# A soft mixture of experts behind a Fourier layer: the last product on half rows, without zero blocks

## The chip, the core and the metric

The kernel runs on one core of a Trainium2 chip. The core has TensorE (matrix products into PSUM), VectorE, ScalarE and GpSimd (elementwise work; GpSimd is POOL in the profile), and SyncE (SP), from whose queue nearly all DMA transfers are issued here. The engines run side by side and wait for each other on semaphores. The metric is the device time of one execution in microseconds (us); lower is better. The kernel before takes 567.42 us (median of three runs, 566.44 to 567.63).

## The reference

Everything is float32. A Fourier layer comes first; its output is never needed in full, only through the mixture behind it.

```python
X = np.fft.rfft(x, axis=1)                   # x: 8 x 2496 x 256
Yr = Xr @ w_r - Xi @ w_i + b_r
Yi = Xr @ w_i + Xi @ w_r + b_i
Yr, Yi = softshrink(Yr, 0.01), softshrink(Yi, 0.01)
x = np.fft.irfft(Y, n=2496, axis=1).reshape(19968, 256)
logits = x @ phi                             # 32 slots: 8 experts of 4
d = softmax(logits, over tokens)
slot_input = d.T @ x                         # 32 x 256
slot_out[e] = relu(slot_input[e] @ w1[e]) @ w2[e]
c = softmax(logits, over slots)
out = c @ slot_out                           # 19968 x 256
```

The change concerns the last line alone: for each of 19968 tokens, a product of its 32 weights c with the 32 x 256 matrix slot_out.

## The kernel before

For most of its time the kernel works through 8 batches of 2496 tokens: transforms, linear layer, softshrink, logits, and for each batch the weights c, which it writes to device memory (c_dr, batches 0 to 5) or keeps in SBUF (batches 6 and 7). An order by due times on a heap (`at`, `step_to`, `run_until`) decides how the stages of neighbouring batches interleave. Behind the last batch come the two layers of the experts (tiles hps and po) and then the combine, with which the program ends.

The weights for two consecutive tokens lie side by side. c_prep (line 1051) splits a batch's weights into a high part in fp32r, written by ScalarE, and the rest, subtracted by VectorE (tile chl); for a pair of tokens this gives 4 x 32 = 128 values: token 0 high, token 0 low, token 1 high, token 1 low. c_trans (line 1061) transposes them on TensorE (tile pc, 11 groups of at most 117 pairs for each batch, in three steps of 4, 4 and 3) and copies them to the tiles ct. A column of ct is then a pair of tokens, its 128 rows are the values above, and 1248 columns belong to each batch.

The combine walks over 78 blocks of 128 columns (NBLK, line 37). For block j, the 128 columns of ct are the stationary matrix, and two products of 512 columns add up in one PSUM bank, pq: one with rhs[0], the high part of slot_out, one with rhs[1], its low part. Each rhs is 128 x 2 x 256: rows 0 to 63 hold slot_out in columns 0 to 255 and zeros behind, rows 64 to 127 hold zeros and then slot_out, so that columns 0 to 255 of pq are the first token of each pair and 256 to 511 the second. Half of what each product multiplies is zero. PSUM banks for pq come by turns from the pools "pf" and "pl", two banks each.

ScalarE copies the even blocks from PSUM to half of a tile ost, VectorE the odd ones to the other half; there are nine buffers for ost. SyncE writes two blocks at a time to the output, 512 KB, and the first two and last two blocks by themselves, 256 KB each (lines 1198 to 1201).

Between the blocks the loop carries work for later batches: the table todo (line 1176) holds for a block which c_prep and c_trans are recorded behind it, and run_until (line 1202) does the same with the steps for the weights of batch 7. Each engine executes its instructions in the order recorded, so a transpose that waits for its chl holds up the products behind it on TensorE.

Before the loop, lines 1160 to 1173 make rhs: po is split into so[0] and so[1], a product with a mask (prep) puts slot_out onto all rows, and copies of 64 rows each put it into rhs over zeros, which GpSimd wrote at lines 1084 to 1087.

Of the kernel before, what the change touches and what calls it, by code (L numbers as in the profile page):

```python
# [11 lines left out]
F32 = mybir.dt.float32  # L12
F32R = mybir.dt.float32r
# [4 lines left out]
B, N, D = 8, 2496, 256  # L18
# [9 lines left out]
E, F = 8, 1024  # L28
# [7 lines left out]
TR = 128  # L36
NBLK = B * CB // TR
# [146 lines left out]
def fourier_soft_moe_kernel(ctx: ExitStack, tc: tile.TileContext, t: dict, out: bass.AP):  # L184
# [18 lines left out]
    def psum(tag, name):  # L203
        return pp.tile([128, 512], F32, tag=tag, name=name, bufs=psum_bufs[tag])

    def wtile(shape, dt, tag, name):
        if tag in a_bufs:
            return wap.tile(list(shape), dt, tag=tag, name=name, bufs=a_bufs[tag])
        if tag in main_bufs:
            return wmp.tile(list(shape), dt, tag=tag, name=name, bufs=main_bufs[tag])  # L210
        return wcp.tile(list(shape), dt, tag=tag, name=name, bufs=chain_bufs[tag])
# [8 lines left out]
    V, A, P = (_InOrder(tc, e) for e in (nc.vector, nc.scalar, nc.gpsimd))  # L220
# [15 lines left out]
    def sp(**kw):  # L236
        tc.keep_in_program_order(nc.sync.dma_start(**kw))
# [4 lines left out]
    def mm(**kw):  # L242
        tc.keep_in_program_order(nc.tensor.matmul(**kw))  # L243

    def copy(eng, out, in_):
        if eng is nc.scalar or eng is A:
            eng.copy(out=out, in_=in_)
        else:
            eng.tensor_copy(out=out, in_=in_)
# [509 lines left out]
    def run_until(t):  # L759
        while heap and heap[0][0] < t:  # L760
            step_to(heapq.heappop(heap)[2])
# [106 lines left out]
    def hl_tile(name):  # L868
        return pools["tm"].tile([128, F], F32, tag="hl", name=name, bufs=NHL)
# [171 lines left out]
    cts, chls = {}, {}  # L1041
# [19 lines left out]
    def c_trans(b, i0, eng):  # L1061
        ni = min(4, G // 2 - i0)
        pc = psum("pt", f"pc{b}_{i0}")
        x, r = divmod(i0, GX // 2)
        for i in range(ni):
            tc.keep_in_program_order(
                nc.tensor.transpose(  # L1067
                    out=pc[:, i * P1 : (i + 1) * P1],
                    in_=chls[b][x][:, 2 * (r + i) : 2 * (r + i) + 2].rearrange("p g h s -> p (g h s)"),
                    identity=ident[:P1, :P1],  # L1070
                )
            )
        c0 = b * CB + i0 * P1
        c1 = min(c0 + ni * P1, (b + 1) * CB)
        for lo in range(c0 - c0 % F, c1, F):
            u0, u1 = max(lo, c0), min(lo + F, c1)
            if lo not in cts:
                cts[lo] = ta_tile(f"ct{lo}").bitcast(F32R)
            copy(eng, cts[lo][:, u0 - lo : u1 - lo], pc[:, u0 - c0 : u1 - c0])
# [1 line left out]
    at(T_["cl"], c_load, 0)  # L1081
    run_until(TB + 24)

    rhs = []
    for a in range(2):
        rhs.append(wtile([128, 2, D], F32R, "p_sb", f"rhs{a}"))
        P.memset(rhs[a].bitcast(F32), 0.0)
    slz, hz = pools["slz"], pools["hz"]
    hps = [psum("pl", f"hps{h}") for h in range(2)]
    po = psum("pr", "po")  # L1090
# [72 lines left out]
    A.copy(out=so[0], in_=po[:, :D])  # L1163
    V.tensor_tensor(out=so[1], in0=po[:, :D], in1=so[0].bitcast(F32), op=ALU.subtract)
    c_trans(0, 0, V)
    for i, tag, dst in ((0, "ps", ((0, A), (1, A))), (1, "pl", ((0, V),)), (1, "pl", ((1, A),))):
        prep = psum(tag, f"prep{i}")
        mm(out=prep[:, :D], lhsT=dmr, rhs=so[i], start=True, stop=True)
        for a, eng in dst:
            r0 = slice(64 * a, 64 * a + 64)  # L1170
            copy(eng, rhs[i][r0, a, :], prep[r0, :D])
    c_trans(0, 4, V)
    c_trans(0, 8, A)

# [1 line left out]
    todo = {}  # L1176
    for b in range(B - 1):
# [2 lines left out]
            todo.setdefault(at0 + 1, []).append((c_prep, b + 1))  # L1180
        for i0, d, eng in ((0, 4, A), (4, 6, V), (8, 8, A)):
            todo.setdefault(at0 + d, []).append((c_trans, b + 1, i0, eng))
    for j in range(NBLK):
        if j % 2 == 0:
            ost = hl_tile(f"ost{j}")
        pq = psum(("pf", "pl")[j % 2], f"pq{j}")
        lo = j * TR - j * TR % F
        for a in range(2):
            mm(
                out=pq,  # L1190
                lhsT=cts[lo][:, j * TR - lo : j * TR - lo + TR],
                rhs=rhs[a].rearrange("p b d -> p (b d)"),
                start=(a == 0),
                stop=(a == 1),
            )
        half = slice(j % 2 * 512, j % 2 * 512 + 512)
        copy((A, V)[j % 2], ost[:, half], pq)
        if j < 2 or j >= NBLK - 2:
            sp(out=out[j // 2, :, half], in_=ost[:, half])
        elif j % 2:  # L1200
            sp(out=out[j // 2], in_=ost)
        run_until(1000 + 6 * j * TR / CB + 0.1)
        for fn, *args in todo.get(j, []):
            fn(*args)


def OUT_SHAPE():
# [55 lines left out]
```

## Time and profile before

| | us |
|---|---|
| Median of three runs | 567.42 |
| The profiled execution | 563.34 |
| Its span, first to last instruction | 561.5 |
| TensorE busy, over the span | 521.4 |
| VectorE busy | 422.0 |
| ScalarE busy | 298.1 |
| GpSimd busy | 281.1 |

A row of the chain of waits gives a start in us, a time in us and the work (engine, tile, line of the code, count of instructions). In the rows of instruction groups stand line, engine, operation, tiles out<-in, shape, count, busy us and mean ns of one, then the idle time of the engine ahead of them with what ended it. Most work carries the line of a helper (L180, L243), so groups are told apart by tiles. The name pq occurs twice: as a tile of the earlier stages (pq<-rt, pq<-pk) and as the bank of the combine (pq<-rhs,ct). "PEld" is the weight load of a product, and a matmul's "mean ns" is its latency: the pace of a series is its time in the chain divided by its count.

### The profile page before, as it was taken

The numbers are of one execution on the slowest core, as the hardware profiler recorded it, in microseconds if no ns is written. First come the engines' busy times: TensorE is split into PE (matmuls) and PEld (weight loads), VectorE is DVE, ScalarE is ACT, GpSimd is POOL, SyncE is SP. The second block draws the span as 40 slices with busy tenths as digits, with TensorE's granted clock in tenths as the row PEclk, the third lists the DMA queues.
The fourth block names the chain that finished last, engine by engine and source line by source line (L and its number), as shares of the span: only waits on it lengthen the run. The fifth ranks groups of instructions, "written<-read, shape, count | busy, mean of one in ns | idle before, by whom it ended". The sixth has DMA issues, their size and how long they took to land.

```text
span 561.5 us, 11780 instructions
## 1 busy us (share of the span) xinstructions
PE 521.4 (93%) x4354; PEld 442.2 (79%) x4354; DVE 422.0 (75%) x837; ACT 298.1 (53%) x650; POOL 281.1 (50%) x258
## 2 busy tenths in 40 slices
PE   8669999999999999999999999999899979899794
PEld 4458999989898889889988898987687867367573
DVE  0347897799979897989789978986795764248783
ACT  4435555666566656665665666653433333147572
POOL 0037777766766576658655866684554402000100
PEclk9999999999999999999999999999999998999899
DMA  8788464756476637664757474766634378979898
GB/s 301 249 294 292 151 207 152 210 179 170 163 216 207 189 118 208 207 180 167 204 171 199 155 201 167 222 230 178 186 131 126 113 183 276 392 240 368 325 374 351
DMA packets 93684, 121.44 MB, mean 216 GB/s; under 512 B 46786, under 2 KB 68736, under 8 KB 93628
## 3 DMA queue, kind: packets, MB, share of 16 engines
q1 hardware_dynamic: 93372, 119.63, 65.4%
q10 hardware_dynamic: 256, 1.08, 0.5%
q8 instruction: 34, 0.56, 0.4%
q14 instruction: 22, 0.18, 0.1%
HBM read 69.87 MB, written 50.82 MB: 215 GB/s over the span
## 4 chain that ended last, share of the span: by engine, by line
PE 70%; DVE 13%; DMA 10%; ACT 3%; issue 2%; SPq 1%; ACTq 0%; DVEq 0%
PE py L243 16%; PE px L243 11%; PE pq L243 9%; PE pa L243 8%; PE pk L243 7%; PE pt L532 4%; PE pr L243 3%; DMA eb<-ed 2%; PE pc L1067 2%; DMA ad<-ast 2%; PE pe L243 2%; DMA ap<-adr 2%; DVE mx L180 1%; DVE clpL L180 1%; DVE xtl L180 1%
## 5 line engine op out<-in xcount | busy, mean ns | idle before, releaser
L180 POOL TENSOR_TENSOR rt<-ut,rt 128x512 f32<-128x512 f32 x79 | 111.7, 1414 | 24.4 <-DVE rt L180 18.4
L180 POOL TENSOR_TENSOR xsl<-xsm,xsh 128x256 fp32r<-128x256 f32 x77 | 59.3, 770 | 102.4 <-DVE xsh L180 71.0
L180 POOL TENSOR_TENSOR xl<-xr,xh 117x512 fp32r<-117x512 f32 x73 | 98.5, 1350 | 22.6 <-ACT xh L180 14.7
L243 PE MATMUL px<-smov,ap 128*128 128x128 f32 x640 | 85.6, 277 | 8.0 <-DMA ap<-adr 4.5
L243 PEld LDWEIGHTS px<-smov,ap 128*128 128x128 f32 x640 | 80.3, 193 | 13.7 <-issue 8.1
L180 ACT CAST xth<-px 128x512 fp32r<-128x512 f32 x80 | 46.8, 585 | 73.0 <-PE py L243 37.6
L180 ACT COPY ast<-pa 128x512 f32<-128x512 f32 x86 | 50.3, 587 | 64.5 <-PE pa L243 61.6
L180 DVE SCALAR_TENSOR_TENSOR ut<-py,pk,k 128x256 f32<-128x256 f32 x160 | 69.5, 475 | 15.0 <-PE py L243 13.1
L180 DVE TENSOR_TENSOR xtl<-px,xth 128x512 fp32r<-128x512 f32 x80 | 54.6, 682 | 26.8 <-ACT xsm L180 22.0
L243 PE MATMUL py<-xth,nwsh 128*128 128x256 f32 x160 | 53.5, 334 | 0.0
L180 DVE TENSOR_SCALAR rt<-ut 128x512 f32<-128x512 f32 x69 | 52.2, 756 | 0.5
L243 PE MATMUL pk<-xsh,w_rh 128*128 128x256 f32 x160 | 47.9, 300 | 2.0 <-DVE xsh L180 2.0
L180 ACT COPY T<-pt 128x512 f32<-128x512 f32 x70 | 42.1, 601 | 9.0 <-PE pt L532 7.3
L532 PE MATMUL pt<-pk,rt 128*128 128x128 f32 x320 | 45.9, 273 | 0.9 <-DVE dd L180 0.6
L243 PE MATMUL pk<-xsl,w_rh 128*128 128x256 f32 x160 | 45.1, 282 | 0.0
L243 PE MATMUL pk<-xsh,w_rl 128*128 128x256 f32 x160 | 44.9, 281 | 0.0
L243 PE MATMUL py<-xtl,nwsh 128*128 128x256 f32 x160 | 44.7, 279 | 0.0
L243 PE MATMUL py<-xtl,wdh 128*128 128x256 f32 x160 | 44.7, 279 | 0.0
L243 PE MATMUL py<-xth,wdl 128*128 128x256 f32 x160 | 44.7, 279 | 0.0
L243 PE MATMUL py<-xth,nwsl 128*128 128x256 f32 x160 | 44.7, 279 | 0.0
L243 PE MATMUL py<-xth,wdh 128*128 128x256 f32 x160 | 44.7, 279 | 0.0
L243 PE MATMUL pq<-rhs,ct 128*128 128x512 f32 x156 | 43.1, 415 | 0.3 <-DVE ost L180 0.3
(186 smaller groups left out, 1241.7 us busy)
## 6 DMA issues: line engine op xcount, KB each, us to landing
ap<-adr SPq DMA_DIRECT2D x76, 256.0 KB
out<-ost SPq DMA_DIRECT2D x37, 512.0 KB
xr<-in_x SPq DMA_DIRECT2D x35, 512.0 KB
adr<-ast SPq DMA_DIRECT2D x20, 768.0 KB
w<-in_moe_w SPq DMA_DIRECT2D x25, 512.0 KB
adr<-ast SPq DMA_DIRECT2D x8, 512.0 KB
w<-in_moe_w SPq DMA_DIRECT2D x14, 256.0 KB
x<-in_x SPq DMA_DIRECT2D x11, 256.0 KB
```

The lines of the kernel that those rows point to most:

```text
L180: return lambda *a, **k: self.tc.keep_in_program_order(f(*a, **k))
L243: tc.keep_in_program_order(nc.tensor.matmul(**kw))
L532: tc.keep_in_program_order(nc.tensor.transpose(out=out, in_=in_, identity=identity))
L1067: nc.tensor.transpose(out=pc[:, i * P1 : (i + 1) * P1], in_=chls[b][x][:, 2 * (r + i) : 2 * (r + i) + 2].rearrange("p g h s -> p (g h s)") ...
```

## The change

The loop goes over pairs of blocks (j - 1, j). A pair has two banks, one from "pf" for the first tokens and one from "pl" for the second. For each of the two blocks and each of high and low, there are two products of 64 rows and 256 columns: rows 0 to 63 into the first bank, rows 64 to 127 into the second. A rhs is 128 x 256 without zero blocks. ScalarE copies the first bank and VectorE the second, each to the two places in ost that belong to its tokens. All writes are of 512 KB. What todo holds for either block is recorded behind the pair.

```diff
-    rhs = []
-    for a in range(2):
-        rhs.append(wtile([128, 2, D], F32R, "p_sb", f"rhs{a}"))
-        P.memset(rhs[a].bitcast(F32), 0.0)
+    rhs = [wtile([128, D], F32R, "p_sb", f"rhs{a}") for a in range(2)]
...
-    for i, tag, dst in ((0, "ps", ((0, A), (1, A))), (1, "pl", ((0, V),)), (1, "pl", ((1, A),))):
+    for i, tag, eng in ((0, "ps", A), (1, "pl", V)):
         prep = psum(tag, f"prep{i}")
         mm(out=prep[:, :D], lhsT=dmr, rhs=so[i], start=True, stop=True)
-        for a, eng in dst:
-            r0 = slice(64 * a, 64 * a + 64)
-            copy(eng, rhs[i][r0, a, :], prep[r0, :D])
+        copy(eng, rhs[i], prep[:, :D])
...
-    for j in range(NBLK):
-        if j % 2 == 0:
-            ost = hl_tile(f"ost{j}")
-        pq = psum(("pf", "pl")[j % 2], f"pq{j}")
-        lo = j * TR - j * TR % F
-        for a in range(2):
-            mm(
-                out=pq,
-                lhsT=cts[lo][:, j * TR - lo : j * TR - lo + TR],
-                rhs=rhs[a].rearrange("p b d -> p (b d)"),
-                start=(a == 0),
-                stop=(a == 1),
-            )
-        half = slice(j % 2 * 512, j % 2 * 512 + 512)
-        copy((A, V)[j % 2], ost[:, half], pq)
-        if j < 2 or j >= NBLK - 2:
-            sp(out=out[j // 2, :, half], in_=ost[:, half])
-        elif j % 2:
-            sp(out=out[j // 2], in_=ost)
+    for j in range(1, NBLK, 2):
+        ost = hl_tile(f"ost{j}")
+        ov = ost.rearrange("p (k g d) -> p k g d", g=2, d=D)
+        pqs = [psum(tag, f"pq{j}_{g}") for g, tag in enumerate(("pf", "pl"))]
+        for k in range(2):
+            c = (j - 1 + k) * TR
+            lo = c - c % F
+            for a in range(2):
+                for g in range(2):
+                    rows = slice(64 * g, 64 * g + 64)
+                    mm(
+                        out=pqs[g][:, k * D : k * D + D],
+                        lhsT=cts[lo][rows, c - lo : c - lo + TR],
+                        rhs=rhs[a][rows],
+                        start=(a == 0),
+                        stop=(a == 1),
+                    )
+        for g in range(2):
+            copy((A, V)[g], ov[:, :, g, :], pqs[g].rearrange("p (k d) -> p k d", d=D))
+        sp(out=out[j // 2], in_=ost)
         run_until(1000 + 6 * j * TR / CB + 0.1)
-        for fn, *args in todo.get(j, []):
-            fn(*args)
+        for i in (j - 1, j):
+            for fn, *args in todo.get(i, []):
+                fn(*args)
```

On TensorE before, at the third pair of blocks, where the first transposes of batch 1 stand (names as above, with buffer numbers):

```order
L243 MATMUL pq_7009<-rhs_6797,ct_6962 128x512
L243 MATMUL pq_7009<-rhs_6799,ct_6962 128x512
L1067 MATMUL pc_0_7013<-pk_112,chl_0_6913 128x117 x4
L243 MATMUL pq_7019<-rhs_6797,ct_6962 128x512
L243 MATMUL pq_7019<-rhs_6799,ct_6962 128x512
```

The same place on TensorE after the change:

```order
L243 MATMUL pq_0_7010<-rhs_6797,ct_6960 128x256
L243 MATMUL pq_1_7011<-rhs_6797,ct_6960 128x256
L243 MATMUL pq_0_7010<-rhs_6798,ct_6960 128x256
L243 MATMUL pq_1_7011<-rhs_6798,ct_6960 128x256
L243 MATMUL pq_0_7010<-rhs_6797,ct_6960 128x256
L243 MATMUL pq_1_7011<-rhs_6797,ct_6960 128x256
L243 MATMUL pq_0_7010<-rhs_6798,ct_6960 128x256
L243 MATMUL pq_1_7011<-rhs_6798,ct_6960 128x256
L1067 MATMUL pc_0_7023<-pk_112,chl_0_6911 128x117 x4
```

Four products of 512 columns became eight of 256, whose outputs alternate between the two banks, and the transposes that stood between the blocks of a pair stand behind it.

On VectorE before, around the split of batch 2 (chl):

```order
L180 COPY ost_7042<-pq_7052 128x512
L180 TENSOR_TENSOR chl_0_7062<-cin_6853,chl_0_7062 117x16x32
L180 TENSOR_TENSOR chl_1_7065<-cin_6853,chl_1_7065 117x6x32
L180 COPY ost_7057<-pq_7068 128x512
L180 COPY ost_7074<-pq_7079 128x512
```

The same place on VectorE after the change:

```order
L180 COPY ost_7051<-pq_1_7053 128x2x256
L180 COPY ost_7070<-pq_1_7072 128x2x256
L180 TENSOR_TENSOR chl_0_7085<-cin_6851,chl_0_7085 117x16x32
L180 TENSOR_TENSOR chl_1_7088<-cin_6851,chl_1_7088 117x6x32
L180 COPY ost_7091<-pq_1_7093 128x2x256
```

The split moved behind the copy of its pair; the number of copies did not change.

## The prediction

> **What bounds the kernel now.** The diff touches the last stage alone, so I first read the chain of work that ended last, from 440 us on. The columns are the start, the time and the work. These rows open and close the stage.
>
> ```profile
> 500.50 0.51 PE prep L243 x2
> 501.00 0.70 PE pc L1067 x7
> 501.71 2.32 PE pq L243 x10
> ...
> 548.48 5.08 PE pq L243 x22
> 553.56 0.02 issue
> 553.58 0.69 DVE ost L180
> ```
>
> The combine runs from 501.71 to 554.27 us and TensorE carries most of the chain. Yet the span ends at 561.5, seven microseconds behind the last copy. So I went on to the output queue: SyncE's own timeline, and the busy time by stretch.
>
> ```profile
> 502.83 0.36 SPq L237 DMA_DIRECT2D out<-ost  x1
> 534.21 0.93 SPq L237 DMA_DIRECT2D out<-ost  x2
> 553.89 3.68 SPq L237 DMA_DIRECT2D out<-ost  x3
> core 0: us, PE busy (x) PEld busy (x) DVE busy (x) ACT busy (x) POOL busy (x), PEclk, DMA share, GB/s
> 503.90:514.00 10.10, 9.48 (x54) 7.60 (x53) 7.90 (x17) 7.45 (x15) 1.26 (x1) 1.00 0.88 350
> 514.00:524.00 10.00, 8.01 (x40) 5.76 (x38) 8.16 (x12) 6.64 (x15) 1.49 (x2) 1.00 1.00 399
> 524.00:535.00 11.00, 9.39 (x42) 7.20 (x43) 8.62 (x16) 6.11 (x14) 1.38 (x1) 0.84 0.66 264
> 535.00:559.00 24.00, 18.07 (x93) 14.14 (x91) 15.34 (x27) 12.99 (x26) 0.00 (x0) 1.00 1.02 404
> ```
>
> From 535 us on the queue moves 404 GB/s at a share of 1.02: it is full, and the last three writes need 3.68 us to be issued, until 557.57, though the last copy is done at 554.27. Before 535 it starves. The missing part is (404 - 350) / 404 of 10.1 us, (404 - 399) / 404 of 10 and (404 - 264) / 404 of 11, that is 1.35 + 0.12 + 3.81 = **5.3 us**. A write of two blocks is 512 KB, 0.524 MB, so 1.30 us at 404 GB/s. Counting pairs from 0, the first write was issued at 502.83 and pair 20 would have to be issued by 502.83 + 20 x 1.30 = 528.8 to leave no hole. It was issued at 534.21, 5.4 us late, which is the same loss seen from the other side. Behind that pair compute gains on the queue, and its time is hidden.
>
> So the stage is bound by compute up to pair 20 and by the output queue behind it. The change can win 5.3 us at most, and only by what it saves before 535. In that part, these are the waits of VectorE and of TensorE (502 to 535 us: total, times, longest).
>
> ```profile
> DVE ost L180 <- PE pq L243: 4.7, 9, 1.2
> DVE chl L180 <- ACT chl L180: 1.9, 3, 0.9
> PE pc L1067 <- DVE chl L180: 3.9, 4, 1.9
> ```
>
> VectorE is busy 7.90 + 8.16 + 8.62 = 24.7 of 31.1 us, TensorE 26.9. VectorE's idle time is 4.7 us for products and 1.9 us for ScalarE's split of a batch (chl). TensorE's idle time is its wait for VectorE's half of that split.
>
> **The change part by part: the products.** Here are the operations now, over the stage (line, engine, names, count, busy time, mean ns, idle before).
>
> ```profile
> L243 PE MATMUL pq<-rhs,ct 128*128 128x512 f32 x156 | 43.1, 415 | 0.3 <-DVE ost L180 0.3
> L243 PEld LDWEIGHTS pq<-rhs,ct 128*128 128x128 f32 x156 | 28.3, 195 | 6.0 <-DVE ost L180 1.1
> L180 DVE COPY ost<-pq 128x512 f32<-128x512 f32 x39 | 26.3, 684 | 8.3 <-PE pq L243 8.1
> L180 ACT COPY ost<-pq 128x512 f32<-128x512 f32 x39 | 22.8, 587 | 11.8 <-PE pq L243 9.9 <-ACT ct L180 1.0 <-DVE ost L180 0.6
> ```
>
> The mean of 415 ns is a latency; the pace is 5.08 us / 22 = 231 ns, so a pair of blocks takes 4 x 231 = 0.92 us. After the change a pair is eight products of 256 columns, each with its own weight load of 128 columns over 64 rows. No product in the trace uses half of the rows, so its price has to be bounded from the nearest rows.
>
> ```profile
> 446.15 2.91 PE py L243 x24
> 450.59 2.09 PE pq L243 x16
> 452.98 0.44 PE pt L532 x4
> 468.69 1.44 PE pe L243 x4
> 493.37 6.18 PE po L243 x112
> ```
>
> py is the same width (256 moving columns, 128x128 weights, fp32r): 2.91 / 24 = 121 ns each. If two halves do not overlap, a product costs that, and a pair 8 x 121 = 0.97 us: 0.05 us more than now. The pq row at 450.59 is another tile of that name, with 32 moving columns only, and still takes 2.09 / 16 = 131 ns; transposes of 128 columns take 0.44 / 4 = 110. A fresh weight load of 128 columns is therefore worth 110 to 131 ns by itself when it cannot run beside another load, and products that overlap while their loads do not are no cheaper than 110 ns. For overlap speaks po: four column groups of 32 into one bank, 256 columns, 6.18 / 112 = 55 ns each, 0.22 ns per column, where pe on the full array takes 1.44 / 4 = 360 ns for 352 columns, 1.02 ns per column. Parts of the array do run side by side in this kernel, by columns. So the ends are 60 ns a product (two at a time, 121 / 2) and 131. I take **60**, since po is the only row with a divided array and shows all of the overlap, and keep 110 to 131 as the rival. A pair then takes 0.48 us.
>
> On the load the Trainium skill has rules for both sides. "TensorE: Matmul & The Clock Gate", section LDWEIGHTS, says that loading time depends on the columns and not on the rows; the 110 ns of the transposes agree, and by that rule alone the doubled loads would make this change a loss (the rival below, 570.9). "TensorEngine Tiling (Array Packing)", section Key Properties, says that different tiles can load and multiply in parallel; no run so far shows two row halves, and by it the forecast stands.
>
> **The change of shape.** Products on half rows now alternate with the full-array transposes (pc). The nearest row is transposes put between products on column groups.
>
> ```profile
> 489.26 0.68 PE pht L532 x4
> ...
> 492.66 0.71 PE pht L532 x4
> ```
>
> They take 0.70 us for four, against 0.44 for pt: 0.25 us for both switches. I take 0.25 for each group of pc; the ends are 0 and 0.27. There are 12 such groups up to pair 20 (three for each of four batches), 3.0 us of TensorE time. With 0.48 us a pair, TensorE needs 21 x 0.48 + 44 x 0.10 + 3.0 = 17.5 us where VectorE needs 24.7, so most is hidden; it shows where VectorE waits anyway, behind the four splits: 4 x 0.25 = **1.0 us**. The same page of the Trainium skill says in that section that a change of tiling mode drains TensorE. The pht rows agree; were it not so for row halves, the sum would be better by this 1.0 us.
>
> **The rest.** Number and size of the copies stay: 39 on ScalarE and 39 on VectorE, their output now in two runs of 256. These two groups read the same 512 columns in runs of 64.
>
> ```profile
> L180 ACT CAST xth<-px 128x512 fp32r<-128x512 f32 x80 | 46.8, 585 | 73.0 <-PE py L243 37.6
> L180 DVE TENSOR_TENSOR xtl<-px,xth 128x512 fp32r<-128x512 f32 x80 | 54.6, 682 | 26.8 <-ACT xsm L180 22.0
> ...
> 515.74 0.96 DVE L180 TENSOR_TENSOR chl<-cin,chl 117x512 fp32r<-117x512 f32 x2 [0.79 <-ACT chl L180]
> ```
>
> They take 585 and 682 ns, against 587 and 684 for the copies: the runs cost 0. Both copies of a pair now start together, so the pair is complete 0.69 us behind its last product, as before. VectorE's half of a batch's split (0.96 us) now stands behind the copy of its pair, not ahead of it: that write goes 0.96 us earlier and the transposes that wait for the split come 0.69 later. For the queue one is worth the other; I take 0, with these two as the ends.
>
> The preparation loses one of three prep products and two of four half copies: 0.51 / 2 = 0.25 us less on the chain, down to a ct copy that pair 1 needs from VectorE. But the first write is now 512 KB and waits for the whole pair, where 256 KB went at 502.83. I put the two at 0, ends -0.25 and +0.4. The memsets on GpSimd lie far from the chain: 0. At the end, one write of 512 KB replaces two of 256; the queue is full there, so 0, and up to +0.6 if the queue should run dry.
>
> **The clock.** In 524 to 535 the granted clock was 0.84. The chain shows what that cost.
>
> ```profile
> 524.41 0.71 PE pc L1067 x4
> 525.12 1.73 PE pq L243 x4
> ...
> 527.62 1.25 PE pq L243 x4
> ...
> 541.07 0.94 PE pq L243 x4
> ```
>
> Four products took 1.73 and 1.25 us, not 0.94: 1.1 us. This followed TensorE's longest wait (1.9 us for chl), whose causes, ScalarE's and VectorE's splits with a GpSimd subtraction beside them, stay. I leave that **1.1 us** in.
>
> **The sum.** VectorE can gain its 4.7 us of waits for products, less 1.0 for switches and 1.1 for the clock: **2.6 us** of the 5.3 us of starving. Behind 535 nothing is won. The profiled execution took 563.34 us (1.84 around its span) and would take 560.7. The median of the runs shown is 567.42, 4.08 above it; I carry that difference over, since nothing before 499 us moves: **564.8 us**, 0.5% faster. Its own range goes from a gain of 4.4 (hardly any switch or clock loss) to one of 1.0 (two more stretches at half clock): 563.0 to 566.4.
>
> **The rivals.**
> *Loads do not overlap; slower.* Place: TensorE's weight loads, eight of 128 columns in a pair where four were. Price at 121 ns a product: 21 pairs x 0.05 = 1.0 us, 3.0 for the switches, now in the open, 0.46 us more at each of the four splits, since both banks of a pair are complete only at its end (1.8), and 0.4 at the first write: 6.2. TensorE's idle 4.2 us (31.1 - 26.9) takes up part; between 2.0 and 6.2 I take 3.5: **570.9 us**. For it: the 110 and 131 ns rows. Against it: po. It decides from about 100 ns a product, where 21 x (0.92 - 0.80) = 2.5 us pays for what is left of the switches and of the pairing.
>
> *The gain is eaten.* Products at 85 to 95 ns, or VectorE still late for other reasons: it has 24.7 us of work of its own up to 535, and pair 20 is due at 528.8, 26 us behind the first write. Then 4.7 shrinks to about 2.6 while the 2.1 stay: 0.5 us, **566.9 us**. For it: VectorE's 79% in these stretches, and the queue that hides all behind pair 20. Against it: its waits for products are the largest.
>
> **How the numbers follow.** A measurement of this kernel can tell about 0.2%, 1.1 us, from no change. Forecast 0.52 (0.42 faster, 0.09 within, 0.01 slower); loads that do not overlap 0.32 (0.03, 0.04, 0.25); eaten 0.16 (0.03, 0.08, 0.05). Together 0.48 faster, 0.21 the same, 0.31 slower. The range must reach into the slower case: 563.0 to 571.3 leaves out half of it, 0.16, and little below.
>
> **What would show it.** Right: 312 products whose eight take about 0.48 us in the chain; VectorE's waits for pq before 535 near 1 us; a queue near 400 GB/s from 504 on, with the last copy well before 552. Wrong: products 110 ns or more apart, TensorE without idle time through the stage, pc groups of four that take 0.65 us rather than 0.40, and 264 GB/s or less around 530.

## The result, and the profile after

The changed kernel takes 569.67 us (median of 11 runs, 569.09 to 573.43), the kernel before 566.44 (11 runs, 564.31 to 567.83). The ratio is **1.0082**, 95% interval 1.0057 to 1.0107: 0.8% slower, where 0.5% faster was forecast. A second series gave 1.0028 (0.9991 to 1.0065), so the size of the loss is less sure than the first interval says; the forecast gain lies outside both.

The ends of the stage in the chain of waits of the changed kernel, and its output queue, in one row for all writes:

```profile
500.72 0.39 PE prep L243
501.11 0.70 PE pc L1067 x7
501.81 0.72 PE pq L243 x7
...
559.34 0.69 DVE ost L180
```

```profile
503.30 59.79 SPq L237 DMA_DIRECT2D out<-ost  x39
```

The start is as before, but the last copy ends at 560.03, not 554.27. By stretch (the columns are those of the table before, the granted clock stands third from the end):

```profile
503.90:514.00 10.10, 7.98 (x68) 6.19 (x67) 7.46 (x15) 6.28 (x12) 1.37 (x1) 0.82 0.92 365
514.00:524.00 10.00, 8.75 (x66) 6.78 (x64) 5.73 (x10) 5.63 (x12) 0.00 (x0) 0.67 0.78 315
524.00:535.00 11.00, 9.95 (x72) 7.97 (x69) 7.97 (x11) 6.28 (x14) 1.70 (x1) 0.54 0.71 287
...
535.00:559.00 24.00, 19.61 (x176) 15.13 (x172) 18.01 (x33) 14.45 (x30) 1.37 (x1) 0.86 0.80 319
559.00:569.00 10.00, 0.27 (x6) 0.06 (x2) 0.69 (x1) 0.58 (x1) 0.00 (x0) 0.62 0.73 288
```

The reader is to see two columns. The queue, full from 535 on before, now has a share of 0.80 there: 0.64 from 535 to 547 and 0.96 from 547 to 559, so it starves through most of the stage. And the granted clock, 1.00, 1.00 and 0.84 before in the first three stretches, is 0.82, 0.67 and 0.54. Over the combine, from the first prep product at 500.35 to the last copy, its mean is 0.77; as every record of it in these traces is either 1 or a half, that is 2 x 0.23 x 59.7 = 27 us at half clock, against 3 before. What grants the clock is called the clock gate below, and closed where it grants a half.

The profiled execution is no exception. Each timed run has its mean clock over the span, and the median is 0.969 and 0.964 in the two series of the changed kernel, but 0.980 to 0.984 in the three series of the old one beside the later runs.

The waits from 502 to 535 us, the groups of the stage, and the group of pc before the change:

```profile
DVE ost L180 <- PE pq L243: 8.0, 14, 1.2
...
PE pc L1067 <- DVE chl L180: 4.4, 3, 2.1
```

```profile
L243 PE MATMUL pq<-rhs,ct 64*128 64x256 f32 x312 | 34.5, 356 | 1.1 <-ACT ost L180 1.0
L243 PEld LDWEIGHTS pq<-rhs,ct 64*128 64x128 f32 x312 | 27.5, 239 | 7.8 <-ACT ost L180 5.0 <-issue 0.9
L180 DVE COPY ost<-pq 128x512 f32<-128x512 f32 x39 | 26.4, 687 | 13.2 <-PE pq L243 13.1
L180 ACT COPY ost<-pq 128x512 f32<-128x512 f32 x39 | 22.4, 587 | 16.5 <-PE pq L243 14.5 <-ACT ct L180 1.3 <-ACT ost L180 0.4
L1067 PE MATMUL pc<-pk,chl 117*128 117x117 f32 x88 | 18.0, 340 | 7.9 <-DVE chl L180 7.9
```

```profile
L1067 PE MATMUL pc<-pk,chl 117*128 117x117 f32 x88 | 13.3, 273 | 4.4 <-DVE chl L180 4.4
```

The copies cost what they did. VectorE waits longer for products in the part that decides (8.0 us, before 4.7), and TensorE waits 7.9 us for the splits over the stage (before 4.4), though its products are cheaper. Up to 535 its wait has grown only from 3.9 to 4.4 us, so the wait alone is not the loss. Its chain shows what comes behind it:

```profile
504.58 0.67 PE pq L243 x8
505.25 0.55 PE pc L1067 x4
...
506.92 0.72 PE pq L243 x8
507.63 0.57 ACT ost L180
508.21 0.69 ACT cb L180
508.90 0.52 ACT chl L180
509.41 0.02 issue
509.44 0.70 DVE chl L180
510.14 0.04 issue
510.18 1.00 PE pc L1067 x4
511.18 1.15 PE pq L243 x5
512.34 0.97 PE pc L1067 x4
...
515.24 2.62 PE pq L243 x23
517.86 0.03 ACTq L180
...
519.20 0.62 PE pc L1067 x4
```

The same place in the chain before the change:

```profile
509.95 0.59 PE pc L1067 x4
510.54 0.94 PE pq L243 x4
...
513.12 2.50 PE pq L243 x10
515.62 0.03 ACTq L180
...
516.58 0.59 PE pc L1067 x4
```

TensorE has finished its pairs by 508 and stands before the transposes of the next batch, whose split comes only behind ScalarE's copies and VectorE's. Counted from the first prep product, these transposes begin at 9.83 us, and at 9.82 before the change: the shorter products bring the split no earlier, and TensorE only waits longer for it. After that wait everything on it takes twice as long. At full clock four transposes take 0.55 us in this profile and eight products behind them 0.67; here 0.97 to 1.00 and 1.15 (the row at 511.18 names five of its eight products). So the transposes of the next split begin at 18.85 us where they began at 16.45. Of these 2.4 us 2.0 are TensorE's own: to the ACTq row it needs 7.7 us for five pairs, where it needed 5.7 for four and a half.

The first prep product starts between 500.1 and 509.7 us in the profiles below, although nothing ahead of it differs from one kernel to the next but two memsets of rhs on GpSimd. So the stage is compared from there, and the verdicts rest on the ratios of the timed runs. Three profiles (pairs_full, after_again, grouped_early) are of executions over 1.5% above the fastest of their kernel.

| kernel | ratio to before (95%) | prep to last copy, us | granted clock there | prep to end, us |
|---|---|---|---|---|
| before | 1 | 54.1 | 0.97 | 61.4 |
| changed | 1.0082 (1.0057 to 1.0107) | 59.7 | 0.77 | 68.8 |
| changed, again | 1.0028 (0.9991 to 1.0065) | 57.1 | 0.82 | 66.1 |
| pairs_full | 1.0037 (1.0000 to 1.0074) | 54.5 | 0.97 | 61.9 |
| dummies8 | 1.0089 (1.0054 to 1.0123) | 58.7 | 1.00 | 65.7 |
| dummies4 | 1.0064 (1.0030 to 1.0098) | 55.0 | 0.97 | 62.8 |
| grouped | 0.9995 (0.9963 to 1.0028) | 51.0 | 0.93 | 59.8 |
| full_grouped | 1.0005 (0.9977 to 1.0034) | 52.6 | 1.00 | 59.3 |
| early | 0.9967 (0.9943 to 0.9991) | 49.3 | 0.90 | 58.5 |
| early, again | 0.9943 (0.9921 to 0.9966) | 48.3 | 0.93 | 57.8 |
| before_early | 1.0000 (0.9972 to 1.0028) | 52.9 | 0.97 | 60.5 |
| full_early | 0.9936 (0.9913 to 0.9958) | 48.4 | 1.00 | 57.2 |
| grouped_early | 1.0016 (0.9989 to 1.0043) | 54.4 | 0.91 | 63.3 |

### The profile page after: what moved, and what is told of

Its sections match the earlier page's. It is cut to its first block, busy times and chain, and to the rows that moved or that the text cites. A ratio compares the mean times of both kernels' runs of the same rounds, so it can differ in the third digit from the quotient of the medians.

```text
span 569.1 us, 12074 instructions
## 1 busy us (share of the span) xinstructions
PE 524.1 (92%) x4509; PEld 444.7 (78%) x4509; DVE 423.3 (74%) x837; ACT 297.3 (52%) x648; POOL 280.6 (49%) x256
## 4 chain that ended last, share of the span: by engine, by line
PE 69%; DVE 13%; DMA 9%; ACT 4%; issue 2%; SPq 1%; POOL 0%; ACTq 0%; DVEq 0%
PE py L243 15%; PE px L243 10%; PE pa L243 8%; PE pq L243 8%; PE pk L243 7%; PE pt L532 4%; PE pr L243 3%; PE pc L1067 3%; DMA eb<-ed 2%; DMA ap<-adr 2%; PE pe L243 1%; PE pg L243 1%; DVE xtl L180 1%; PE hps L243 1%; DMA gp<-gd 1%
## 5 line engine op out<-in xcount | busy, mean ns | idle before, releaser
L180 POOL TENSOR_TENSOR xsl<-xsm,xsh 128x256 fp32r<-128x256 f32 x77 | 59.3, 770 | 103.9 <-DVE xsh L180 73.2
L180 ACT COPY ast<-pa 128x512 f32<-128x512 f32 x86 | 50.5, 587 | 64.3 <-PE pa L243 62.8
L532 PEld LDWEIGHTS pt<-pk,rt 128*128 128x128 f32 x320 | 36.5, 140 | 5.2 <-ACT T L180 1.1
```

The costliest lines, as they stand in the source:

```text
L180: return lambda *a, **k: self.tc.keep_in_program_order(f(*a, **k))
L532: tc.keep_in_program_order(nc.tensor.transpose(out=out, in_=in_, identity=identity))
```

## The experiments

### Pairs without half rows

pairs_full has the order, the pairs and the writes of the changed kernel, but whole-row products and the rhs with zero blocks:

```diff
+                mm(out=pqs[k], lhsT=cts[lo][:, c - lo : c - lo + TR],
+                   rhs=rhs[a].rearrange("p b d -> p (b d)"), start=(a == 0), stop=(a == 1))
...
+        for k in range(2):
+            copy((A, V)[k], ost[:, k * 512 : k * 512 + 512], pqs[k])
```

> Full-row products of 512 columns with the zero blocks, but in pairs of blocks, with writes of 512 KB and the later work recorded behind a pair. Theory clock (the change is slow because TensorE, less busy, is held at half clock for 27 of the 57 us of the combine): granted clock about 0.95 in the combine and 566 to 568 us, within 0.3% of before. Theory switches (the drains at 21 groups of transposes): the same, since no switch is left. Theory pairing (both banks of a pair are ready late, and the transposes come later): slower than before by 0.4% or more, 569 us or above.

The stage takes 61.9 us, 0.5 more than before, at a clock of 0.97. The ratio, 1.0037, leaves room for a loss by the pairing of up to 0.7%, but its profile shows little of one. In the profiles, what separates it from the changed kernel's 68.8 and 66.1 us is the half rows: the transposes of the first and the next split begin 6.6 us apart here (520.36 and 526.99), as before the change, and 9.0 in the changed kernel. By the ratios alone it cannot be told from the second series of the changed kernel (1.0028), so how much of the loss is the pairing's stays open. The half clock is not the pairing's: the median clock of the timed runs is 0.980 here, as in the old kernel.

### More work on TensorE

Eight or four further products behind each pair, into banks that nobody reads:

```diff
+        for i in range(8):
+            g = i % 2
+            mm(out=dum[g][:, :D], lhsT=cts[lo][64 * g : 64 * g + 64, c - lo : c - lo + TR],
+               rhs=rhs[0][64 * g : 64 * g + 64], start=True, stop=True)
```

> The changed kernel with eight further half-row products behind each pair, into two banks that nobody reads: twice the product work on TensorE, 0.48 us more a pair, 18.7 us in all. Theory clock: the granted clock of the combine goes from 0.75 to 0.95 or more, the extra work is paid back, and the time is not above the changed kernel's 569.7, 565 to 569.5. Theories switches and pairing: the extra work comes on top wherever TensorE is waited for, 572 us or more.

> The same with four further products behind each pair, 0.24 us, 9.4 us in all. Theory clock: part of the windows at half clock go, clock 0.80 to 0.95, 566 to 570 us. Theories switches and pairing: 570 to 573 us.

```profile
520.22 0.48 PE pq L243 x8
520.70 0.48 PE dum L243 x8
521.17 0.52 PE pq L243 x8
```

These rows of dummies8's chain give the price of a half-row product at full clock: 0.48 / 8 = 60 ns. With 18.7 us more on TensorE the clock stays at 1.00, and the stage takes 65.7 us, less than the changed kernel's 68.8 and 66.1; with 9.4 us more, 62.8. The medians are 570.73 us, between what the clock (up to 569.5) and the other theories (572 or more) had asked for, and 568.31, inside the clock's range and below that of the others. The ratios, 1.0089 and 1.0064, stand beside 1.0082 and 1.0028 without the work: by them the extra work costs between nothing and 0.6%, and by the clock column and the stage it pays for itself. So filling TensorE's idle time brings the clock back, in the timed runs too (median 0.984). It does not bring back the old time, as the extra work itself is on the chain (PE dum, 22.9% of it from 520 to 545; 65.7 us for the stage against 61.4): what the half clock alone costs cannot be read from here.

### Fewer changes of shape

```diff
-        for i0, d, eng in ((0, 4, A), (4, 6, V), (8, 8, A)):
+        for i0, d, eng in ((0, 5, A), (4, 5, V), (8, 5, A)):
```

> The changed kernel with the three groups of transposes of a batch recorded behind one pair, so 7 changes of shape and back in place of 21. The page of the changed kernel shows 0.55 us for four transposes in place of 0.40 and 0.67 us for the products behind them in place of 0.48, 0.34 us a group. Theory switches: 14 x 0.34 = 4.8 us less on TensorE, 565 to 567.5 us. Theory clock: the idle time and so the windows at half clock stay, 568.5 to 571 us. Theory pairing: no change, 569 to 570.5 us.

> Full-row products in pairs, with the three groups of transposes of a batch behind one pair: the control for the run that grouped them with half rows (59.8 us from prep to the end, against 68.8). Theory switches: grouping saves nothing here, since there is no change of shape, 61 to 63 us (61.9 without grouping). If grouping helps by the order alone: 59 to 60.5 us.

With half rows the stage falls to 59.8 us and the ratio to 0.9995. The median, 565.05 us, is what the theory of the switches had asked for, but the stage falls by more than its 4.8 us, and the clock, which was to stay, rises from 0.77 to 0.93. With whole rows grouping gives 59.3 us, which the theory of the switches excluded: 2.6 us come from the order alone. Of the 6 to 9 us that grouping saves with half rows in the profiles, then, 4 to 6 belong to half rows. By the ratios it is less: grouping brings 1.9 to 4.9 us with half rows and 1.8 with whole ones.

### A series without waits

Behind the last product, TensorE runs series into banks that nobody reads:

```diff
+    whole(160)
+    one_side(170)
+    whole(120)
+    two_sides(320)
+    whole(120)
+    for _ in range(17):
+        turn(4)          # four transposes
+        two_sides(8)
+    whole(120)
+    for _ in range(16):
+        turn(4)
+        whole(8)
+    whole(60)
```

> The changed kernel, and behind its last product on TensorE a series without any wait, into two banks that nobody reads: 160 whole products of 256 columns, 170 half-row products on rows 0 to 63 alone, 120 whole, 320 half-row products by turns on both halves, 120 whole, 17 times (4 transposes, 8 half-row products), 120 whole, 16 times (4 transposes, 8 whole products), 60 whole. Theory clock, in the form that the gate counts how much of the array works: full clock in the whole products, half clock in the one-sided series and perhaps in the turns with transposes, full clock in the two-sided one. Theory that only waiting closes the gate: full clock through all of the series; then the half clock in the changed kernel comes from its waits alone. Prices: a turn of 4 transposes and 8 half-row products 1.22 us at full clock if switches cost 0.34 us, 0.88 if they cost nothing.

```profile
576.70:597.20 20.50, 20.50 (x171) 20.41 (x170) 0.00 (x0) 0.00 (x0) 0.00 (x0) 1.00 0.00 1
...
611.90:631.10 19.20, 19.20 (x320) 19.16 (x320) 0.00 (x0) 0.00 (x0) 0.00 (x0) 1.00 0.01 3
...
645.70:666.30 20.60, 20.60 (x206) 15.82 (x204) 0.00 (x0) 0.00 (x0) 0.00 (x0) 1.00 0.00 1
...
680.90:701.60 20.70, 20.70 (x185) 20.70 (x184) 0.00 (x0) 0.00 (x0) 0.00 (x0) 1.00 0.01 2
```

A turn is four transposes and the eight products behind them. The rows are, by stretch, the one-sided series, the two-sided one, the turns with half rows and the turns with whole rows. The clock is 1.00 in all: half-filled rows do not close an open gate, nor do switches. The form in which the gate counts how much of the array works has fallen; waits are left. Prices: 19.2 / 320 = 60 ns for two-sided products, 120 for one-sided. A turn takes 20.6 / 17 = 1.21 us, and its parts without switches 4 x 0.10 + 8 x 0.06 = 0.88: **0.33 us for both switches**. With whole rows the chain shows 1.37 us from one turn to the next, and 4 x 0.10 + 8 x 0.121 is as much: no change of shape, no cost.

### The changed kernel again, and the split four blocks earlier

```diff
-            todo.setdefault(at0 + 1, []).append((c_prep, b + 1))
+            todo.setdefault(at0 - 3, []).append((c_prep, b + 1))
```

> The changed kernel once more, for the spread of its clock. Theory clock: the windows at half clock are not a chance of one execution, 15 us or more of them in the combine, and from the first prep product to the end 66 to 70 us (68.8 in the first profile, 61.4 before the change). If that was a chance: under 10 us of half clock and 62 to 65 us.

> The changed kernel with the split of a batch (c_prep) recorded four blocks earlier, so that the transposes find it done; the switches stay at 21. Theory clock: TensorE's waits of 7.9 us for the split go, fewer windows at half clock (under 14 us of 27), 64 us or less from prep to the end. Theory switches alone: 1 to 3 us less than the changed kernel, 66 to 68 us. Theory pairing: the pairs find their transposes in time again, near 62 us.

The second profile of the changed kernel has a clock of 0.82, 2 x 0.18 x 57.1 = 21 us at half: so it was not the chance of one execution. The runs gate and gate2 hold the same stage with other work behind it, and there the clock is 0.85 and 0.74, 17 and 31 us at half. In all four profiles the first split's transposes begin 9.83 or 9.84 us behind the first prep product. With the early split the wait of TensorE for chl is gone from the list, the stage falls by 7.6 to 10.3 us to 58.5, and the kernel is 0.33% faster than before, with all 21 groups still in place. That is below what pairing or switches alone allowed. TensorE now waits 4.4 us for copies instead, and the clock is about half of the way back: 0.90 in the stage, and a median of 0.977 in the timed runs.

### The early split and its controls

> The changed kernel with the split four blocks earlier, again, beside its controls on one chip. Theory waits (with the shorter products TensorE comes to the transposes before the split is done, waits, and its clock is halved behind the wait): 0.3% faster than before the change once more, 57 to 60 us from the first prep product to the end. If the first result was a chance: within 0.2% of before.

> The kernel before, with the split four blocks earlier: the control. Theory waits: the old kernel waits less for the split (3.9 us up to 535), so it gains less than the changed kernel did (68.8 and 66.1 to 58.5 us): 0 to 3 us, 58.5 to 61.5 us from prep to the end. If the early split is all of the gain and half rows bring nothing: as fast as the early split with half rows, or faster.

> Full-row products in pairs with the early split: half rows against whole rows at the same order of work. Theory waits: half rows are now the better by 0 to 2 us, this one 58.5 to 61 us from prep to the end. Theory switches: whole rows are the better, as 21 x 0.34 = 7.1 us of switches weigh more than what half rows save: 56 to 58 us.

> The changed kernel with both, the early split and the three groups of transposes behind one pair. Theory waits together with switches at 0.34 us: at the limit that the output queue sets, 56 to 58.5 us from prep to the end, 0.3 to 0.8% faster than before. If grouping makes a new wait (the third group needs a bank that the first group's copy frees): 58.5 to 60 us.

The gain of the early split held (0.9943). The old loop gains nothing by it (1.0000). But whole rows in pairs with the early split are as fast as half rows, 0.9936 against 0.9943, and have the shorter stage: the expectation that half rows would win by 0 to 2 us was a miss, and 57.2 us is what the theory of the switches had asked for. The stretches of early_again show why there is little left to win:

```profile
514.00:524.00 10.00, 8.59 (x85) 6.31 (x82) 8.76 (x17) 7.23 (x17) 1.37 (x1) 1.00 1.02 401
524.00:535.00 11.00, 9.47 (x75) 7.19 (x74) 8.71 (x17) 7.56 (x17) 2.75 (x2) 0.80 1.02 404
```

The output queue is full from 514 to 535, and so some 20 us sooner than before, even with some half clock. Why pairs gain by the early split and the old loop does not was not tried apart; in the list of before_early TensorE waits 3.6 us for VectorE's copies, in that of full_early 0.3. grouped_early is a miss for both theories (63.3 us, 1.0016): TensorE waits for copies of both engines there, 8.2 us; which of them is at fault stays open.

### What keeps the clock at half

In the changed kernel the clock stayed at half in windows that TensorE filled. The edges below are those at which the clock changed, or may change, 3.41 us apart:

```profile
506.85:510.27 3.42, 1.30 (x18) 1.10 (x18) 1.90 (x4) 3.08 (x7) 0.00 (x0) 1.00 1.02 406
510.27:513.68 3.41, 3.41 (x20) 2.59 (x22) 3.01 (x8) 1.14 (x2) 1.22 (x1) 0.50 0.89 356
513.68:517.09 3.41, 3.41 (x27) 2.76 (x25) 1.70 (x3) 1.59 (x3) 0.15 (x1) 0.50 0.68 271
517.09:520.50 3.41, 2.16 (x23) 1.66 (x22) 2.32 (x5) 2.45 (x6) 0.00 (x0) 1.00 0.82 327
520.50:523.90 3.40, 3.40 (x21) 2.59 (x23) 2.03 (x3) 1.59 (x3) 0.00 (x0) 0.50 0.81 327
```

A window in which TensorE was busy 1.30 us is followed by half clock; one filled with turns, 510 to 513.7, by half clock again. A last kernel puts series behind waits of 6 us, twice over, without a wait inside:

```diff
+    for rep in range(2):
+        idle(9, 3 * rep)             # ten copies on ScalarE, then one product
+        for _ in range(16):
+            turn(4)
+            two_sides(8)
+        whole(100)
+        idle(9, 3 * rep + 1)
+        for _ in range(14):
+            turn(4)
+            whole(8)
+        whole(60)
+        idle(9, 3 * rep + 2)
+        two_sides(320)
+        whole(60)
```

> The changed kernel, and behind its last product, twice over, three series that each follow a wait of TensorE of about 5 us (ten copies on ScalarE), which should close the gate: 16 times (4 transposes, 8 half-row products); 14 times (4 transposes, 8 whole products); 320 half-row products without transposes. Whole products stand between them. Theory A, the drains at the changes of shape keep a closed gate closed: the first series stays at half clock for two windows of 3.4 us or more, some or all of its turns at about 2 us in place of 1.22, while the second and the third are back at full clock after one window. Theory B, one busy window opens the gate whatever fills it: all three are back at full clock after at most 3.4 to 6.8 us, and the many windows at half clock of the changed kernel come from its later waits.

```profile
584.15:607.50 23.35, 23.35 (x193) 17.87 (x192) 0.00 (x0) 0.00 (x0) 0.00 (x0) 0.80 0.01 1
626.20:646.40 20.20, 20.20 (x160) 20.20 (x160) 0.00 (x0) 0.00 (x0) 0.00 (x0) 0.88 0.01 2
661.30:682.20 20.90, 20.90 (x321) 20.84 (x320) 0.00 (x0) 0.00 (x0) 0.00 (x0) 0.91 0.01 2
696.16:721.20 25.04, 25.04 (x193) 19.19 (x192) 0.00 (x0) 0.00 (x0) 0.00 (x0) 0.74 0.01 1
739.92:759.60 19.68, 19.68 (x160) 19.68 (x160) 0.00 (x0) 0.00 (x0) 0.00 (x0) 0.91 0.01 2
774.56:795.10 20.54, 20.54 (x321) 20.54 (x320) 0.00 (x0) 0.00 (x0) 0.00 (x0) 0.93 0.01 2
```

The rows are the series in order. Half clock is twice what is missing from 1, times the length: 9.3 and 13.0 us for the turns with half rows (first and fourth row), 4.8 and 3.5 for the turns with whole rows, 3.8 and 2.9 for half rows without turns. Counted from one change of the clock to the next, it is at half for four and five windows of 3.41 us there (579.65 to 593.31 and 692.29 to 709.36), and for two at each of the other four series, the end of each wait included. So neither half rows nor transposes alone hold the clock down, but turns between them do, for two to three windows more. This is what theory A asked for; that the drains are the reason was not tried apart. The Trainium skill, "TensorE: Matmul & The Clock Gate", Part 1, says that one busy window brings back full clock; the second, third, fifth and sixth row agree, the first and the fourth do not (two and three windows that TensorE filled went by at half clock), and the measurement decides.

## Why the prediction was wrong

**What bounds the kernel: right.** Compute ahead of about 535 us decides, and the output queue sets the limit: with the early split the queue is full from 514 to 535 and the time falls.

**Products on half rows: right.** 60 ns was forecast, 60 ns was measured in dummies8 and gate. Two row halves load and multiply side by side, and the rival with loads that do not overlap has fallen, although its 570.9 us lies near the result: the time came out near it by another mechanism. The 110 ns of the transposes, whose loads fill all rows, could not have told between the two. That the stated range, 563.0 to 571.3, holds the 569.67 us is luck, as its upper part stood for this rival.

**Switches: right in kind, too small.** 0.25 us a group was forecast, from transposes between column groups; the turns of gate show 0.33, a third more. Over 21 groups that is 7 us. The products save 39 x (0.92 - 0.48) = 17 us of TensorE's time at full clock, so the balance of TensorE's time was still good by 10 us.

**The clock: the step that failed.** The prediction put "I leave that **1.1 us** in", what one stretch at half clock cost the old kernel, and went down to "two more stretches at half clock" for its range. The old kernel had one window of 3.41 us at half in the stage; the changed one had eight and six in its two profiles, 27 and 21 us. The runs show two conditions for it. A TensorE that is done sooner waits longer for a split whose time ScalarE and VectorE set (9.83 us behind the first prep product, before 9.82), and behind the wait the gate is closed: with less of the wait (early) or with idle time filled (dummies8) the clock comes back in part or in full, and without waits it never falls (gate). Then the turns keep it closed (gate2). Both belong to the change: shorter products lengthen the wait, and half rows make the turns a change of shape.

**VectorE's waits for products: wrong for the same reason.** The sum took 4.7 us of them off; up to 535 they grew to 8.0. At half clock a turn costs TensorE about 2.1 us (0.97 and 1.15 in the chain), more than at full clock in the old kernel (0.40 and 0.92). Between the first two splits 2.0 us of the loss are TensorE's own work, most of it at half clock and with its switches; how the whole loss divides between the longer wait, the clock, the switches and the pairing was not measured separately.

**Copies, prep and the first write:** ScalarE and VectorE copies at 587 and 687 ns as forecast. The first write is issued 2.95 us behind the first prep product (500.35 to 503.30), before 2.70: 0.25 us, inside its bounds of -0.25 and +0.4.

**What was missing from the sum** is an event behind the saving: who waits when TensorE is early. The row was there, 3.9 us of TensorE's waits for chl, together with the stretch at 0.84 that followed; the prediction kept both as they were, when the change lengthened the one and multiplied the other. The later place of the split, which it put at 0, cost 0.01 us at the first split.

## What to carry to other kernels

Make an engine faster only after looking at what it waits for next: here the next wait, with the half clock behind it, took back all that the faster products brought, and in the loop over pairs moving the awaited work four blocks ahead was worth more than the change itself (0.9943 and 0.9936, with and without half rows). Where products on part of the array alternate with whole-array work, count about a third of a microsecond for each round trip, gather the whole-array work, and look at the granted clock by stretch, not at the mean of the span (0.960 against 0.77 in the stage). And where a queue sets the limit of the stage, compare a clever form with the plain one at the best order: whole rows in pairs with the early split, at 0.9936, are as fast as anything that was run.

## What the runs showed of the hardware that was not expected

Two products on 64 rows each, in two halves of the array and into two banks, run fully side by side with their weight loads: 60 ns a product of 256 columns, 120 on one half alone. A closed clock gate can stay closed while TensorE is fully occupied without any wait, if the work alternates between half-row products and whole-array transposes: 9.3 and 13.0 us, against 2.9 to 4.8 for the other series. Each such turn costs 0.33 us for its two changes of shape. And the same instructions ahead of the combine brought its start anywhere from 500.1 to 509.7 us in these profiles, more than the change itself moves; only the length of the stage could be compared from one profile to another.
